# Another order for the attention blocks, other owners for the zeroing, and later stores, in an attention and mixture-of-experts kernel

## The chip, the cores and the metric

The program runs on one core of one Trainium2 chip. The metric is the device time of one execution in microseconds (us). A change is called faster or slower from 0.5% on, which is 4.5 us here.

## What is computed

The reference is an attention over short windows, a mixture of eight experts with a greedy assignment, and a gated network. Shapes: 4 batches, 8 heads, 768 positions, 64 elements in a head; 3072 tokens of 512 elements; expert width 1024.

```python
for c in range(24):                       # chunks of 32 queries
    k_full = concat([mem_k, k[16 to the left .. 8 to the right of the chunk]])   # 64 keys
    a = softmax(scale * q_c @ k_full.T)
    out[chunk] = a @ v_full
x = out.transpose(0, 2, 1, 3).reshape(3072, 512)
...
logits = x @ w_gate                       # pairs (token, expert) taken in falling order,
...                                       # each expert takes 384 tokens
for e in range(8):
    out[mask] = relu(x[mask] @ w1[e]) @ w2[e]
...
h = (x @ w1) * (x @ w2) @ w3
out = h @ w_out
```

## The kernel before

**Stages.** Attention comes first. It is cut into 32 units; unit u is half of a group g = u // 2 (one batch, one pair of heads, three tiles of 128 queries). One unit is a score block on TensorE (L298, 12 matmuls of 32 output partitions each), a maximum and a subtraction on VectorE (L308 to L312), an exponential on ScalarE (L316), a block of three transposes (L324) and its copy (L331), a value block (L341, again 12 matmuls of 32 output partitions), a division (L349 to L351), and a second block of three transposes with a copy (L324, L358). When four units have been done, a logit block follows (L372, 4 matmuls of 32 output partitions, and L381, three transposes). Score, value and logit blocks use 32 columns of the array, four blocks of columns side by side (column-tiled); transposes and all other matmuls use the full 128. A fp32 matmul of these blocks appears twice in the trace, so that a block of 12 is a row x24.

Then the tokens are assigned to experts (`route`, one pass for each expert: VectorE compares with thresholds, L569, and TensorE counts, L634 and L641). Beside the first pass TensorE multiplies `w3` with `w_out` ahead of time: 192 matmuls (L486, called combine matmuls here; 24 for each of 8 results) whose operands come from a conversion of 16 `w3` loads and 8 `w_out` loads on ScalarE and VectorE (L445 to L466). The first pass ends in a list of tokens; GpSimd gathers their rows (L812), and the eight experts follow one behind the other (L472 to L474 and L910 to L959).

**What sets the order.** `Plan` is a list scheduler that runs when the program is built. Each task asks for an engine ("P" TensorE, "V" VectorE, "A" ScalarE, "G" GpSimd, "D" the DMA issues of SyncE), a planned duration and an earliest time; `run` takes the task that could start first, by its own clock, and emits it. The order of the instructions on every engine is fixed by that. The planned durations have no other effect.

**Buffers and queues.** Keys lie in `kd0` to `kd2`, values in `vd0` to `vd2`, queries in `a5` to `a7`, for group g in buffer g % 3. The key and value buffers hold zeros outside two diagonal blocks, written once by memsets (L232). All loads and stores that matter here are issued by SyncE in order. `w3` blocks are loaded into `a6`, `a7`, `a5` (once the last scores of that query buffer are done) and into `a0` to `a4` (once the last logits are done). `stores` writes the attention's result to memory (`xs`), 24 stores of 128 tokens, from where it is gathered.

Of the kernel before, what the change touches and what calls it, by code (L numbers as in the profile page):

```python
# [11 lines left out]
I32 = mybir.dt.int32  # L12
# [48 lines left out]
GROUPS = B * HP  # L61
UNITS = 2 * GROUPS


class Slots:

# [30 lines left out]
class Plan:  # L97
# [8 lines left out]
    DMA = 2.3  # L106
    BIAS = 1.0

    def __init__(self):
        self.free = {e: 0.0 for e in "PVAGD"}  # L110
        self.at, self.tasks = {}, []

# [15 lines left out]
    def run(self):  # L128
        while self.tasks:
            ready = []  # L130
            for t in list(self.tasks):
                if t[2] is None:
                    self.step(t, None)
                if t[2] is None:
                    continue
                engines, held, _, after = t[2]
                held = held if isinstance(held, tuple) else (held,)
                e, h = min(zip(engines, held), key=lambda x: max(self.free[x[0]], after + self.LATENCY) + x[1] + (self.BIAS if x[0] == "V" else 0.0))
                ready.append((max(self.free[e], after + self.LATENCY), t[0], e, h, t))
            first = min(ready, key=lambda r: r[:2])  # L140
            same = [r for r in ready if r[2] == first[2] and r[0] <= first[0] + (self.SLACK if r[1] == 50.0 and r[2] == "V" else 0.0)]
            start, _, e, h, t = min(same, key=lambda r: (r[1], r[0]))
            emit = t[2][2]
            emit(e) if isinstance(t[2][1], tuple) else emit()
            self.free[e] = start + h
            self.step(t, start + h + (self.DMA if e == "D" else 0.0))


class Net:
# [78 lines left out]
    def zeros(self):  # L228
        nc = self.nc

        def zero(t, s):
            return lambda e: (nc.vector if e == "V" else nc.gpsimd).memset(t[:, s], 0.0)  # L232

        for i in range(3):
            for n, t in (("zk", self.KD[i]), ("zv", self.VD[i])):
                c = t.shape[2] * (t.shape[3] if len(t.shape) > 3 else 1) / 960
                t0 = yield ("VG", (c, c), zero(t, 0), 0.0)
                t1 = yield ("VG", (c, c), zero(t, 1), 0.0)
                self.at[n, i] = max(t0, t1)

    def loads(self):
        nc, io = self.nc, self.io

        def keys(g):
            b, hp = divmod(g, HP)
            if g >= 3:
                yield from self.wait(("s", 2 * g - 5))
            r = yield from self.wait(("zk", g % 3))

            def k():  # L250
                for s in range(2):
                    nc.sync.dma_start(self.KD[g % 3][s::2, s], io["kT"][b, hp, s])

            yield from queries(g) if g < 3 else ()
            t = yield ("D", 1.4, k, r)
            if g < 3:
                self.at["k", g] = t
            else:
                yield from queries(g)

        def values(g):
            b, hp = divmod(g, HP)
            r = yield from self.wait(("zv", g % 3) if g < 3 else ("o", 2 * g - 5))

            def v():
                for s in range(2):
                    nc.sync.dma_start(self.VD[g % 3][s::2, s].rearrange("p c d -> p (c d)"), io["vw"][b, hp, s])

            self.at["v", g] = yield ("D", 2.22, v, r)

        def queries(g):
            b, hp = divmod(g, HP)
            r = (yield from self.wait(("s", 2 * g - 5))) if g >= 3 else 0.0
            self.at["k", g] = yield ("D", 1.09, lambda: nc.sync.dma_start(self.Q[g % 3], io["qT"][b, hp]), r)

# [8 lines left out]
    def unit(self, u):  # L284
# [7 lines left out]
        p = bank[:, :6 * SL].rearrange("p (t h s) -> p t h s", t=3, h=2)  # L292

        def scores():
            for t in range(3):
# [4 lines left out]

        ts = at["s", u] = yield ("P", 0.89, scores, max(t0, tk))
        te, n = yield from self.EX.get()
# [4 lines left out]
        def top():  # L307
# [7 lines left out]
        P = self.P[n_P]  # L315
        t = yield ("A", 0.41, lambda: nc.scalar.activation(  # L316
            P.rearrange("p t (s h) -> p t h s", h=2), self.ex[n].rearrange("p (t h s) -> p t h s", t=3, h=2), AF.Exp, scale=0.125),
# [17 lines left out]
        o = bank[:, :6 * VW].rearrange("p (t h d) -> p t h d", t=3, h=2)  # L335

        def values():
            for t in range(3):
# [4 lines left out]

        t = at["o", u] = yield ("P", 0.89, values, max(t, to, tv))
        self.PTT.put(n_T, t)
# [16 lines left out]
    def logits(self, b, hf):  # L362
# [5 lines left out]
        tb, p = yield from self.R.get()  # L368

        def first():  # L370
            for k in range(HP):
# [18 lines left out]
    def stores(self, b, hf):  # L390
        t = yield from self.wait(*[("x", 2 * (HP * b + hp) + hf) for hp in range(HP)])
        for j in range(3):
            r = b * S + (3 * hf + j) * 128
# [33 lines left out]
    def fetch(self, jobs, *first):  # L427
        nc = self.nc
        yield from self.wait(*first)
        for n, tag, src, keys in jobs:  # L430
            t = yield from self.wait(*keys)
            raw = self.raw[n] = tag, self.place(tag, [1024], I32)
            self.at["raw", n] = yield ("D", 1.46, lambda: nc.sync.dma_start(raw[1], src.bitcast(I32)), t)

# [656 lines left out]
```

## Time and profile before

| | |
|---|---|
| median of 3 runs | 896.81 us (895.02 to 898.84) |
| profiled execution | 893.84 us, span 892.1 us |
| TensorE busy | 862.7 us (97% of the span) |
| VectorE busy | 579.7 us (65%) |
| ScalarE busy | 346.5 us (39%) |
| GpSimd busy | 65.3 us (7%) |

The span is the time from the first to the last instruction in the trace; the profiled execution is the same run with what lies around it. In the trace PE is TensorE, PEld its weight loads, DVE VectorE, ACT ScalarE, POOL GpSimd and SPq the DMA issues of SyncE. Ends of matmuls are modelled, so where one block follows another the start-to-start distance says what the first cost.

### The profile page before, as it was taken

Reading aid. Unit: us, or ns where it says so; the run is one execution under the profiler, and the core shown is the slowest. Engines: PE = TensorE matmul, PEld = TensorE weight load, DVE = VectorE, ACT = ScalarE, POOL = GpSimd, SP = SyncE. Lnnn points to the kernel's source line nnn. Section 1 sums busy time; section 2 is a strip of 40 time slices with the busy share of each in tenths; the row PEclk is TensorE's granted clock in tenths of the full one; section 3 lists DMA queues with packets and bytes.
Section 4 is the critical chain, followed back from the end, with each engine's and each line's share of the span. In section 5 each row is a group of like instructions: output and inputs, shape, how many; then the busy total and the mean of one; then the engine's idle time right before and its main releaser. Section 6 shows DMA issues by size and latency. Waiting matters only on the chain.

```text
span 892.1 us, 16212 instructions
## 1 busy us (share of the span) xinstructions
PE 862.7 (97%) x6561; PEld 776.5 (87%) x6561; DVE 579.7 (65%) x1321; ACT 346.5 (39%) x609; POOL 65.3 (7%) x88
## 2 busy tenths in 40 slices
PE   7999999899989999999999999999999999999996
PEld 6777667798979988998999999989999999999995
DVE  6889788697858856885779477857851175213211
ACT  3778796796223312331133113221341134113211
POOL 3000000000100010101011001100110011001001
PEclk9999999999999999999999999999999999999999
DMA  8999792850522160326023402530250024003000
GB/s 300 411 346 396 277 366 82 309 213 1 163 68 105 60 169 1 107 72 159 1 106 113 117 1 107 151 79 1 84 177 1 1 105 155 1 1 107 1 1 35
DMA packets 36267, 110.36 MB, mean 124 GB/s; under 512 B 9440, under 2 KB 9952, under 8 KB 35552
## 3 DMA queue, kind: packets, MB, share of 16 engines
q1 hardware_dynamic: 32352, 96.74, 31.6%
q0 software_dynamic: 3840, 12.59, 4.4%
q8 instruction: 51, 0.84, 0.4%
q14 instruction: 24, 0.20, 0.1%
HBM read 96.24 MB, written 13.07 MB: 123 GB/s over the span
## 4 chain that ended last, share of the span: by engine, by line
PE 78%; DVE 10%; DMA 7%; POOL 1%; issue 1%; ACT 1%; SPq 0%; POOLq 0%; DVEq 0%; ACTq 0%
PE bank L910 9%; PE bank L472 9%; PE bank L918 9%; PE bank L911 9%; PE bank L473 9%; PE bank L474 9%; PE bank L951 5%; PE bank L959 5%; PE bank L952 5%; DMA x<-xs,ix 4%; PE bank L486 3%; PE bank L634 2%; PE bank L324 1%; DVE kd L398 1%; DVE ex L756 1%; DMA a<-in_qT 1%
## 5 line engine op out<-in xcount | busy, mean ns | idle before, releaser
L472 PE MATMUL bank<-x,kd 128*128 128x384 f32 x512 | 175.8, 343 | 0.1
L473 PE MATMUL bank<-x,kd 128*128 128x384 f32 x512 | 172.5, 337 | 1.2 <-DVE kd L398 1.2
L474 PE MATMUL bank<-x,kd 128*128 128x384 f32 x512 | 172.3, 337 | 0.0
L936 DVE TENSOR_TENSOR pt<-pt,bank 128x384 f32<-128x384 f32 x64 | 35.3, 552 | 111.2 <-PE bank L918 104.2
L473 PEld LDWEIGHTS bank<-x,kd 128*128 128x128 f32 x512 | 96.5, 189 | 2.9 <-DVE kd L398 2.3
L472 PEld LDWEIGHTS bank<-x,kd 128*128 128x128 f32 x512 | 96.6, 189 | 1.1 <-ACT x L832 0.4
L474 PEld LDWEIGHTS bank<-x,kd 128*128 128x128 f32 x512 | 96.4, 188 | 0.3 <-DVE x L398 0.3
L666 DVE TENSOR_SCALAR_CACHE_REDUCE ex<-cv,thf 128x1536 bf16<-128x1536 f32 x50 | 90.4, 1809 | 0.3
L910 PE MATMUL bank<-x,a 128*128 128x384 f32 x256 | 87.9, 343 | 0.0
L929 ACT ACTIVATE pt<-bank 128x384 f32<-128x384 f32 x64 | 31.5, 492 | 145.3 <-PE bank L918 142.1
L910 PE MATMUL bank<-x,b 128*128 128x384 f32 x256 | 87.4, 341 | 0.0
L911 PE MATMUL bank<-x,a 128*128 128x384 f32 x256 | 86.0, 336 | 0.0
L911 PE MATMUL bank<-x,b 128*128 128x384 f32 x256 | 85.8, 335 | 0.0
L940 ACT ACTIVATE x<-pt 128x384 fp32r<-128x384 f32 x64 | 33.5, 524 | 123.0 <-DVE pt L936 120.7
L951 PE MATMUL bank<-vd,x 128*128 128x512 f32 x192 | 77.3, 402 | 0.4 <-ACT x L940 0.4
L952 PE MATMUL bank<-vd,x 128*128 128x512 f32 x192 | 75.9, 395 | 0.0
L959 PE MATMUL bank<-vd,x 128*128 128x512 f32 x192 | 66.6, 400 | 0.1
L873 ACT ACTIVATE x<-bank 128x384 fp32r<-128x384 f32 x64 | 31.3, 490 | 86.3 <-PE bank L474 78.5
L812 POOL DMA_INDIRECT x<-xs,ix x24 | 31.1, 1295 | 403.6 <-DVE e L593 143.4
L398 DVE TENSOR_TENSOR kd<-x,kd 128x1024 fp32r<-128x1024 f32 (+1 forms) x38 | 43.2, 1136 | 20.9 <-ACT kd L854 20.8
L918 PE MATMUL bank<-x,a 128*128 128x384 f32 x256 | 56.5, 339 | 0.0
L918 PE MATMUL bank<-x,b 128*128 128x384 f32 x256 | 55.1, 336 | 0.0
(157 smaller groups left out, 1524.1 us busy)
## 6 DMA issues: line engine op xcount, KB each, us to landing
p<-in_w SPq DMA_DIRECT2D x32, 512.0 KB, 3.6
x<-in_w SPq DMA_DIRECT2D x32, 512.0 KB, 3.6
vd<-in_vw SPq DMA_DIRECT2D x32, 390.0 KB, 7.2
a<-in_w SPq DMA_DIRECT2D x16, 512.0 KB, 7.2
kd<-in_kT SPq DMA_DIRECT2D x32, 246.0 KB, 6.2
cv<-vs SPq DMA_DIRECT2D x5, 1536.0 KB, 13.6
a<-in_qT SPq DMA_DIRECT2D x16, 384.0 KB, 6.3
xs<-x SPq DMA_DIRECT2D x24, 256.0 KB, 5.0
```

What stands on the lines that cost most here:

```text
L398: self.nc.vector.tensor_tensor(lo, src, hi.bitcast(F32), op=OP.subtract)
L472: mm(out, sh, mh, start=first, stop=False)
L473: mm(out, sl, mh, start=False, stop=False)
L474: mm(out, sh, ml, start=False, stop=last)
L666: tv = yield ("V", 0.14 + m / 960, lambda: V.tensor_scalar(self.cb[:, :m], self.vt[:, m * i:m * i + m], ti.bitcast(F32), None, op0=OP.is_g ...
L910: mm(q, w[:, 0, 128 * c:128 * c + 128], self.yT[0][:, c], start=(c == 0), stop=False)
L911: mm(q, w[:, 1, 128 * c:128 * c + 128], self.yT[0][:, c], start=False, stop=False)
L918: mm(q, w[:, 0, 128 * c:128 * c + 128], self.yT[1][:, c], start=False, stop=(c == KT - 1))
L936: t = yield ("V", 0.47, lambda: nc.vector.tensor_tensor(self.gf, self.ta, p1[:, :CAP], op=OP.mult), max(t, t1))
L951: mm(p, g[:, 0, r], wc[:, 0], start=(m == 0), stop=False)
L952: mm(p, g[:, 0, r], wc[:, 1], start=False, stop=False)
L959: t = yield ("P", DM * COL, lambda: mm(p, g[:, 1, r], wc[:, 0], start=False, stop=(m == FT - 1)), t1)
```

## The change

Column-tiled emitters get a mark. When the scheduler picks a TensorE task it adds 0.25 us to the start of one that would change between tiled and full (`SWITCH`), and it prefers an attention task (priority under 50) over a later one when that could start within 0.25 us. The planned duration of score and value blocks goes from 0.89 to 0.66, and some planned DMA and exponential durations change. The later key and value buffers are zeroed by GpSimd alone; of the first pair VectorE and GpSimd zero one half each. The stores of batches 1 to 3 wait, in the plan, for the last values' load.

```diff
+def tiled(emit):
+
+    emit.tiled = True
+    return emit
...
+    SWITCH = .25
...
+                turn = self.SWITCH if e == "P" and self.tiled != getattr(t[2][2], "tiled", False) else 0.0
-                ready.append((max(self.free[e], after + self.LATENCY), t[0], e, h, t))
+                ready.append((max(self.free[e], after + self.LATENCY) + turn, t[0], e, h, t))
             first = min(ready, key=lambda r: r[:2])
+            if first[2] == "P" and first[1] > 50.0:
+                first = min((r for r in ready if r[2] == "P" and r[0] <= first[0] + self.SWITCH and r[1] < 50.0), default=first,
+                            key=lambda r: r[:2])
...
-                t0 = yield ("VG", (c, c), zero(t, 0), 0.0)
-                t1 = yield ("VG", (c, c), zero(t, 1), 0.0)
+                t0 = yield ("G" if i else "V", (c,), zero(t, 0), 0.0)
+                t1 = yield ("G", (c,), zero(t, 1), 0.0)
...
-            t = yield ("D", 1.4, k, r)
+            t = yield ("D", 1.3, k, r)
...
-            self.at["v", g] = yield ("D", 2.22, v, r)
+            self.at["v", g] = yield ("D", 2.05, v, r)
...
+        @tiled
         def scores():
...
-        ts = at["s", u] = yield ("P", 0.89, scores, max(t0, tk))
+        ts = at["s", u] = yield ("P", 0.66, scores, max(t0, tk))
...
-        t = yield ("A", 0.41, lambda: nc.scalar.activation(
+        t = yield ("A", 0.48, lambda: nc.scalar.activation(
...
+        @tiled
         def values():
...
-        t = at["o", u] = yield ("P", 0.89, values, max(t, to, tv))
+        t = at["o", u] = yield ("P", 0.66, values, max(t, to, tv))
...
+        @tiled
         def first():
...
         t = yield from self.wait(*[("x", 2 * (HP * b + hp) + hf) for hp in range(HP)])
+        if b:
+            yield from self.wait(("v", GROUPS - 1))
...
-            self.at["raw", n] = yield ("D", 1.46, lambda: nc.sync.dma_start(raw[1], src.bitcast(I32)), t)
+            self.at["raw", n] = yield ("D", 1.35, lambda: nc.sync.dma_start(raw[1], src.bitcast(I32)), t)
```

**TensorE, in the middle of attention.** Before (L298 scores, L341 values, L324 transposes, the bank and the operands behind the name):

```order
L324 MATMUL bank5_106<-ident_73,p_24_99 128x128 x3
L324 MATMUL bank4_105<-ident_73,x2_17_92 128x128 x3
L298 MATMUL bank2_103<-kd1_2_77,a6_13_88 32x128 x12
L324 MATMUL bank5_106<-ident_73,x3_18_93 128x128 x3
L298 MATMUL bank0_101<-kd1_2_77,a6_13_88 32x128 x12
L341 MATMUL bank6_107<-vd0_4_79,pt_25_100 32x130 x12
L324 MATMUL bank4_105<-ident_73,p_24_99 128x128 x3
L324 MATMUL bank5_106<-ident_73,p_24_99 128x128 x3
L298 MATMUL bank1_102<-kd2_3_78,a7_14_89 32x128 x12
L341 MATMUL bank7_108<-vd0_4_79,pt_25_100 32x130 x12
L324 MATMUL bank4_105<-ident_73,x2_17_92 128x128 x3
L324 MATMUL bank5_106<-ident_73,p_24_99 128x128 x3
```

The same place in the changed kernel, where L313 is the score, L357 the value and L339 the transpose line:

```order
L339 MATMUL bank5_106<-ident_73,p_24_99 128x128 x3
L313 MATMUL bank2_103<-kd1_2_77,a6_13_88 32x128 x12
L313 MATMUL bank0_101<-kd1_2_77,a6_13_88 32x128 x12
L357 MATMUL bank7_108<-vd2_6_81,pt_25_100 32x130 x12
L339 MATMUL bank4_105<-ident_73,x3_18_93 128x128 x3
L339 MATMUL bank5_106<-ident_73,x2_17_92 128x128 x3
L339 MATMUL bank4_105<-ident_73,p_24_99 128x128 x3
L339 MATMUL bank5_106<-ident_73,p_24_99 128x128 x3
L313 MATMUL bank1_102<-kd2_3_78,a7_14_89 32x128 x12
L357 MATMUL bank6_107<-vd0_4_79,pt_25_100 32x130 x12
L357 MATMUL bank7_108<-vd0_4_79,pt_25_100 32x130 x12
L313 MATMUL bank2_103<-kd2_3_78,a7_14_89 32x128 x12
```

In the rows of before the array changes between tiled and full 6 times, in those of the changed kernel 3 times; counted over the whole TensorE order there are 86 changes before and 48 now, with the same blocks.

**TensorE, at the end of attention.** Before, from the transposes of the last two units' probabilities on (L486 is the first combine matmul):

```order
L324 MATMUL bank5_106<-ident_73,p_24_99 128x128 x3
L324 MATMUL bank4_105<-ident_73,p_24_99 128x128 x3
L324 MATMUL bank5_106<-ident_73,x6_21_96 128x128 x3
L341 MATMUL bank6_107<-vd0_4_79,pt_25_100 32x130 x12
L324 MATMUL bank4_105<-ident_73,x7_22_97 128x128 x3
L341 MATMUL bank7_108<-vd0_4_79,pt_25_100 32x130 x12
L324 MATMUL bank5_106<-ident_73,x6_21_96 128x128 x3
L486 MATMUL bank2_103<-b0_34_384,kd1_54_1612 128x512 x3
```

And now (L505 is the combine line):

```order
L339 MATMUL bank4_105<-ident_73,p_24_99 128x128 x3
L339 MATMUL bank5_106<-ident_73,p_24_99 128x128 x3
L505 MATMUL bank2_103<-b0_34_378,kd1_52_1524 128x512 x3
L505 MATMUL bank2_103<-b1_36_569,kd1_52_1524 128x512 x2
L339 MATMUL bank4_105<-ident_73,x6_21_96 128x128 x3
L357 MATMUL bank6_107<-vd0_4_79,pt_25_100 32x130 x12
L357 MATMUL bank7_108<-vd0_4_79,pt_25_100 32x130 x12
L339 MATMUL bank5_106<-ident_73,x7_22_97 128x128 x3
```

Five combine matmuls have moved ahead of the last two value blocks. Further on, 18 instead of 16 combine matmuls stand ahead of the last logit transposes (L381), 36 in both ahead of the second count (L634), and 36 instead of 39 ahead of that count's flag (L641); 168 instead of 159 ahead of the second row product (L763) of the first assignment, and 24 instead of 31 between that and the transposes of the gathered rows.

**SyncE, around the last values' load.** Before, from the last values' load to the first `w3` load behind the stores (L267 values, L433 `w3` with its buffer, L394 stores with the tile stored):

```order
L267 DMA vd0_4_79<-in_vw 64x1560 x2
L433 DMA a6_46_1324<-in_w3 128x1024
L433 DMA a7_50_1532<-in_w3 128x1024
L433 DMA a5_51_1566<-in_w3 128x1024
L394 DMA xs_66<-x0_15_90 128x512 x3
L394 DMA xs_66<-x1_16_91 128x512 x3
L394 DMA xs_66<-x2_17_92 128x512 x3
L394 DMA xs_66<-x3_18_93 128x512 x3
L394 DMA xs_66<-x4_19_94 128x512
L433 DMA a0_57_1690<-in_w3 128x1024
```

And now (L281 values, L452 `w3`, L413 stores):

```order
L452 DMA a7_48_1400<-in_w3 128x1024
L281 DMA vd0_4_79<-in_vw 64x1560 x2
L452 DMA a5_50_1470<-in_w3 128x1024
L413 DMA xs_66<-x0_15_90 128x512 x3
L413 DMA xs_66<-x1_16_91 128x512 x3
L413 DMA xs_66<-x2_17_92 128x512 x3
L413 DMA xs_66<-x3_18_93 128x512 x3
L413 DMA xs_66<-x4_19_94 128x512 x3
L413 DMA xs_66<-x5_20_95 128x512 x3
L413 DMA xs_66<-x6_21_96 128x512 x3
L413 DMA xs_66<-x7_22_97 128x512 x2
L452 DMA a0_57_1706<-in_w3 128x1024
```

Two `w3` loads (into `a6` and `a7`) now stand ahead of the last values' load, and 23 stores instead of 13 stand between the load into `a5` and the load into `a0`; the 12 `w3` loads after that follow directly in both, and the stores that are left follow those.

## Rows read from the trace of the kernel before

**Rows 1.** The page's chain that ended last: share of the span by engine.
```profile
PE 78%; DVE 10%; DMA 7%; POOL 1%; issue 1%; ACT 1%; SPq 0%; POOLq 0%; DVEq 0%; ACTq 0%
```

**Rows 2.** Stretches: length, busy us of PE, PEld, DVE, ACT, POOL, granted clock, DMA share, GB/s.
```profile
40.00:60.00 20.00, 19.63 (x423) 15.08 (x419) 17.45 (x57) 16.04 (x33) 0.00 (x0) 1.00 1.01 389
...
100.00:120.00 20.00, 18.53 (x125) 12.67 (x124) 14.20 (x35) 15.75 (x28) 0.00 (x0) 0.91 0.87 337
...
200.00:300.00 100.00, 97.27 (x626) 88.51 (x626) 77.13 (x177) 37.60 (x65) 7.34 (x9) 1.00 0.25 75
```

**Rows 3.** Timeline of PE in attention: start, us, instructions.
```profile
41.14 0.86 PE L298 MATMUL bank<-kd,a 128*32 128x128 f32 x24
41.93 0.55 PE L381 MATMUL bank<-ident,a 128*128 128x128 f32 x3
42.32 0.82 PE L324 MATMUL bank<-ident,x 128*128 128x128 f32 x6
43.06 1.54 PE L341 MATMUL bank<-vd,pt 128*32 128x130 f32 x48
44.42 0.84 PE L298 MATMUL bank<-kd,a 128*32 128x128 f32 x24
```

**Rows 4.** Waits of PEld, 20 to 100 us: total us, times, longest.
```profile
PEld bank L324 <- issue: 3.4, 15, 0.6
...
PEld bank L298 <- issue: 2.9, 17, 0.2
```

**Rows 5.** Timeline of PE at the end of attention, with idle time before.
```profile
97.00 0.52 PE L324 MATMUL bank<-ident,x 128*128 128x128 f32 x3 [1.46 <-DVE small L350]
97.45 0.87 PE L341 MATMUL bank<-vd,pt 128*32 128x130 f32 x24
...
107.00 0.49 PE L381 MATMUL bank<-ident,a 128*128 128x128 f32 x3
```

**Rows 6.** Timeline of SyncE's DMA issues, 79 to 123 us.
```profile
79.63 5.08 SPq L267 DMA_DIRECT2D vd<-in_vw  x4
84.75 7.96 SPq L433 DMA_DIRECT2D a<-in_w  x3
92.75 9.46 SPq L394 DMA_DIRECT2D xs<-x  x13
105.85 16.93 SPq L433 DMA_DIRECT2D a<-in_w  x13
```

**Rows 7.** DMA issues to 170 us: times, KB each, median us to landing.
```profile
vd<-in_vw SPq DMA_DIRECT2D x32, 390.0 KB, 7.2
a<-in_w SPq DMA_DIRECT2D x16, 512.0 KB, 7.2
```

**Rows 8.** Timeline of PE beside the first assignment and at the gather.
```profile
114.78 0.93 PE L634 MATMUL bank<-M,ex 128*63 128x8 bf16 x24 [1.33 <-DVE ex L569]
115.64 1.03 PE L486 MATMUL bank<-b,kd 128*128 128x512 f32 x3
...
151.32 0.46 PE L763 MATMUL bank<-mv,ex 128*128 128x6 bf16 x12
151.64 7.36 PE L486 MATMUL bank<-b,kd 128*128 128x512 f32 x31
...
162.34 1.31 PE L828 MATMUL bank<-ident,x 128*128 128x128 f32 x10 [3.13 <-DMA x<-xs,ix]
```

**Rows 9.** Timeline of DVE: the fourth `w3` block's conversion ends.
```profile
114.65 0.68 DVE L398 TENSOR_TENSOR kd<-cv,kd 128x512 fp32r<-128x512 f32 x1
```

**Rows 10.** Source line of the memsets, then timeline: third key load, its first use.
```profile
L232 POOL MEMSET kd<- x3: 911/911/912, 1.3 to 5.7; 128x984 f32 x3
L232 POOL MEMSET vd<- x3: 1391/1391/1392, 2.1 to 6.5; 128x1560 f32 x3
...
10.15 1.48 SPq L252 DMA_DIRECT2D kd<-in_kT  x2
...
17.10 1.28 PE L298 MATMUL bank<-kd,a 128*32 128x128 f32 x24 [1.97 <-DMA vd<-in_vw]
```

More of the change, by code (lines that the diff above doesn't have):

```diff
@@ L107 @@
     BIAS = 1.0
+    SWITCH = .25
     def __init__(self):
         self.free = {e: 0.0 for e in "PVAGD"}
+        self.tiled = False
         self.at, self.tasks = {}, []
@@ L145, in run @@
             self.free[e] = start + h
+            if e == "P":
+                self.tiled = getattr(t[2][2], "tiled", False)
             self.step(t, start + h + (self.DMA if e == "D" else 0.0))
@@ L273, in queries @@
             r = (yield from self.wait(("s", 2 * g - 5))) if g >= 3 else 0.0
-            self.at["k", g] = yield ("D", 1.09, lambda: nc.sync.dma_start(self.Q[g % 3], io["qT"][b, hp]), r)
+            self.at["k", g] = yield ("D", 1.0, lambda: nc.sync.dma_start(self.Q[g % 3], io["qT"][b, hp]), r)
         yield from keys(0)
```

## Prediction

> **What bounds the kernel now.** I read the chain that ended last first: 78% of it is TensorE [rows 1]. The table of stretches then says where TensorE is short of work: behind the first gather it is busy 97.27 of 100 us and has almost nothing to give [rows 2]. So the change must pay ahead of about 165 us, in attention, beside the first assignment, or at the gather. In attention four things run near their limits together: from 40 to 60 us TensorE is busy 19.63 of 20 us, VectorE 17.45, ScalarE 16.04, and the DMA share is 1.01 [rows 2]. The timeline of TensorE shows what the busy figure hides, the cost of a change between tiled and full blocks [rows 3]. Last come the SyncE issues [rows 6] and the places where TensorE stands still: 1.46 us at the end of attention [rows 5], 1.33 us ahead of the second count, and 3.13 us for the gathered rows [rows 8].
>
> **The change, part by part.** Sums are made against the profiled execution, 893.84 us, which is 3.0 us under the median 896.81; I add the result to the median.
>
> *Fewer changes of tiling: -4.2 us.* In rows 3 two tiled blocks in one row (43.06 to 44.42) take 1.36 us to the next start, so 0.68 each. A tiled block ahead of a full one takes 41.93 - 41.14 = 0.79: the change costs 0.11. Three transposes cost between 0.82 - 0.55 = 0.27 (what three more add to a row) and 42.32 - 41.93 = 0.39 us (from one full block to the next), 0.33 in the middle; the six at 42.32 take 0.74 to the next tiled start, so the change back costs between nothing and 0.20, about 0.10. I take 0.11 for either. The orders have 86 and 48 changes: 38 x 0.11 = 4.2 us. The other end is what the weight loads sit idle: 3.4 / 15 = 0.23 us ahead of full blocks and 2.9 / 17 = 0.17 ahead of tiled ones [rows 4], mean 0.20, or 38 x 0.20 = 7.6 us. Part of that gap lies under the matmuls in flight, and the start-to-start distance holds all that the engine pays, so I take the lower. Below 4.2 us, down to nothing, it falls only if TensorE then waits for loads (rival C).
>
> The Trainium skill, "TensorEngine Tiling", section Tiling Modes, says that a change of mode drains the engine. "TensorE: Matmul & The Clock Gate", section Single matmul latency, gives a constant part of 166 ns for one matmul alone on a warm clock; if a drain costs that, an estimate by this page is 38 x 0.166 = 6.3 us, and the whole sum below would be -3.5 us instead of -1.4. The row shows less than the page's figure, and the sum goes by the row.
>
> *Combine matmuls moved ahead of the last value blocks: -1.2 us.* Before, TensorE waits 1.46 us there for VectorE [rows 5]. Five combine matmuls now stand in that place; one takes 7.36 / 31 = 0.237 us [rows 8], together 1.2 us of work that no longer has to be done later. It needs the first `w3` block early: its load now stands ahead of the last values' load, whose row waits and takes 5.08 us for four issues [rows 6]; two of those are passed, so about 2.5 us earlier. If the block is late, the value blocks queue behind it, and this term turns from a gain of 1.2 into a loss of the same size.
>
> *Stores ahead of most w3 loads: +2.3 us.* SyncE issues in order. Before, 13 stores take 9.46 us, 0.73 each; then the load into `a0` waits until the logits have been read, and goes out at 105.85, 13.1 us behind the end of the load into `a5` at 92.71 [rows 6]. Now 23 stores take 23 x 0.73 = 16.8 us, with no wait for the logits, so `a0` is 3.6 us later measured from `a5`. The load into `a5` waits for the last score block. Between that block and the last logit transposes TensorE now has more to do than before: six transpose blocks and two logit transposes (0.33 each), a value block and a logit block (0.68 each) and two combine matmuls (0.24 each), 4.5 us, less the 1.5 us wait that is filled. So at most 3 us of the 3.6 are made up, and fewer if small waits shrink too, down to about 0.5; I take the middle, 1.8, which leaves 1.8. The fourth `w3` block, out of `a0`, was ready at 114.65 + 0.68 = 115.33, and its first matmul ran at 115.64 [rows 8, 9]: no slack. So these 1.8 us become a wait of TensorE. Two combine matmuls fewer between the last logit transposes and the second count (18, not 20) leave another 0.5 us open, since VectorE's comparison already ends last there (1.33 us) [rows 8]. Queued behind the waiting combine matmul is the third count, so the assignment waits too. Below: nothing, if ScalarE gets through its conversions sooner. Above: rival D.
>
> *Gather: +1.7 us.* From the last row product (151.32 + 0.46 = 151.78) to the gathered rows at 162.34 there are 10.6 us, filled with 31 combine matmuls but for 3.13 us [rows 8]. Now 24 are left to fill it: 7 x 0.237 = 1.7 us more idle. Those matmuls are done earlier, and that time has been counted as work in its new place.
>
> *Zeroing by GpSimd: 0.* GpSimd now clears, from 1.3 us on, five key halves and five value halves; the last key half is done at 1.3 + 5 x 0.91 + 3 x 1.39 = 10.0 us, and the third key load goes out at 10.15 anyway [rows 10]. The second key load cannot go out whole ahead of 1.3 + 3 x 0.91 + 1.39 = 5.4 us, which may hold it by up to 1 us. VectorE is free some 5 us sooner, but TensorE stands still until 17.10 for the loads that follow [rows 10]; that wait covers both a gain and the loss. Without the cover it is worth 1 us either way.
>
> *After the gather: 0.* The work is the same and TensorE is busy 97 of 100 us; the order differs a little in every expert, and I give it 1 us either way.
>
> Sum: -4.2 - 1.2 + 2.3 + 1.7 = **-1.4 us**, 892.4 in a profiled execution, **895.4 us** on the median.
>
> **The rivals.** *B, the full price of a change.* If the idle of the weight loads is what a change costs (7.6 us) and the `w3` blocks arrive in time: -7.6 - 1.2 + 1.7 = -7.1, 889.7 us. For it: the gaps stand in rows 4 under "issue", which waits for nothing else. Against it: the distance of 0.79 us in rows 3.
>
> *C, the loads set attention's pace.* Then the 4.2 us become waits for keys and values: -1.2 + 2.3 + 1.7 = +2.8, 899.6 us. For it: DMA share 1.01 in rows 2, with VectorE at 87%. Against it: the last values were issued by 84.71 us, landed about 7.2 us later at 91.9 [rows 6, 7], and were used at 97.45 [rows 5], 5.5 us of slack that 4.2 us does not use up.
>
> *D, w3 blocks late; the side of slower.* The place is the first matmul out of `a0`. If none of the ten added stores' 10 x 0.73 = 7.3 us is made up, because the stores keep the DMA engines filled and the `w3` loads land only behind them (7.2 us is the median [rows 7]), TensorE waits 7.3 us there. A clock loss comes with it: in the stretch with the 1.33 us wait the granted clock was 0.91 over 20 us, a loss of 1.8 us [rows 2, 8]; one such again. Then -4.2 - 1.2 + 1.7 + 7.3 + 1.8 = +5.4, 902.2 us. It decides (slower by 4.5) from a wait of 6.4 us on. Against it: TensorE's 4.5 us of added work in between.
>
> **How the numbers follow.** The forecast has a chance of 0.42, with a range of its own of 892 to 898.5 us (1 us either way for what follows the gather, and the 0.5 to 3 us above). B has 0.28, C 0.14, D 0.16. A measurement of this kernel tells a change of 0.5%, 4.5 us, from none: under 892.3 is faster, over 901.3 slower. B and 0.05 of the forecast's low tail make 0.33 for faster, D 0.16 for slower, the rest, with C, 0.51 for the same. The range reaches into B and up to C: 889 to 900.5 leaves out about 0.1 of B and most of D, 2 in 10.
>
> **What would show it.** The last logit transposes should start 3 to 6 us ahead of 107.00; a tiled block ahead of a full one should still take 0.79 us. The first combine matmul should start without a wait for its weights. The load into `a0` should go out between 103 and 107 us, and the third count should wait for a combine matmul whose weights VectorE has just written. The wait for the gathered rows should be near 5 us, and they should arrive at 160 to 162 us. The forecast is wrong if attention ends no sooner (C), if it ends 7 us sooner with no wait behind it (B), if the wait at `a0` exceeds 6 us (D), or if experts 1 to 7 differ by more than 1 us together, of which these rows say nothing.

## The result, and the profile after

The changed kernel takes 909.93 us (median of 4 runs, 906.34 to 911.80) against 895.91 us before: ratio 1.0149, 95% interval 1.0105 to 1.0193, 14 us slower. Its profiled execution took 906.34 us, span 904.6 us against 892.1. TensorE was busy 864.8 us (862.7 before): the time was lost in waiting and at a lower granted clock. The traces below are those of these two executions, 12.5 us apart in span.

Stretches of the changed kernel, columns as in [rows 2]:

```profile
40.00:60.00 20.00, 18.89 (x410) 15.40 (x410) 16.83 (x56) 15.25 (x33) 0.00 (x0) 1.00 1.00 394
100.00:120.00 20.00, 18.06 (x179) 11.96 (x174) 12.90 (x37) 12.73 (x24) 0.00 (x0) 0.99 1.02 390
200.00:300.00 100.00, 96.73 (x658) 86.75 (x657) 76.94 (x176) 43.44 (x75) 7.47 (x9) 1.00 0.27 75
...
60.00:70.00 10.00, 7.42 (x149) 6.08 (x145) 6.22 (x17) 5.25 (x11) 0.00 (x0) 0.83 1.01 404
120.00:130.00 10.00, 9.14 (x49) 6.38 (x49) 6.82 (x20) 8.93 (x16) 0.00 (x0) 0.67 1.01 382
165.00:175.00 10.00, 4.85 (x20) 3.84 (x20) 4.08 (x6) 4.04 (x8) 0.95 (x1) 0.66 1.02 410
```

In mid-attention (40 to 60 us) TensorE has lost 0.74 us of work against [rows 2]. In the last three stretches TensorE was busy 9.31, 10.00 and 10.00 us before, at a granted clock of 1.00. One of these losses is in part an old one that moved: before, the clock was low from 110 to 120 us, where it is 0.99 now.

```profile
110.00:120.00 10.00, 8.66 (x68) 6.44 (x66) 8.30 (x20) 9.47 (x16) 0.00 (x0) 0.83 1.00 397
```

TensorE in attention, where [rows 3] showed no gap:

```profile
30.05 1.13 PE L357 MATMUL bank<-vd,pt 128*32 128x130 f32 x30
32.17 0.85 PE L357 MATMUL bank<-vd,pt 128*32 128x130 f32 x18 [0.99 <-issue]
...
46.72 0.87 PE L339 MATMUL bank<-ident,x 128*128 128x128 f32 x6
47.84 0.93 PE L339 MATMUL bank<-ident,p 128*128 128x128 f32 x6 [0.25 <-ACT a L374]
...
60.70 1.47 PE L313 MATMUL bank<-kd,a 128*32 128x128 f32 x42
64.75 0.42 PE L313 MATMUL bank<-kd,a 128*32 128x128 f32 x6 [2.58 <-issue]
```

Two kinds of stop. In the middle of a tiled block TensorE stands still while no semaphore holds it ("issue"): after the 30th of 48 value matmuls, after the 42nd of 48 score matmuls. And of four transpose blocks in a row, on two banks, the third waits until ScalarE has copied the first. TensorE's longest waits from 20 to 110 us:

```profile
PE bank L313 <- issue: 3.6, 2, 2.6
PE bank L339 <- ACT a L374: 2.5, 5, 1.2
PE bank L339 <- ACT pt L346: 2.1, 4, 0.9
PE bank L357 <- issue: 1.0, 1, 1.0
```

Before, the same view had 1.6 us for ScalarE and no "issue" line. SyncE, and TensorE from the end of attention to the gathered rows, in answer to [rows 5, 6, 8]:

```profile
92.84 16.41 SPq L413 DMA_DIRECT2D xs<-x  x23
110.90 13.96 SPq L452 DMA_DIRECT2D a<-in_w  x12
```

```profile
100.68 1.56 PE L505 MATMUL bank<-b,kd 128*128 128x512 f32 x5
...
111.54 0.55 PE L398 MATMUL bank<-ident,a 128*128 128x128 f32 x3
...
118.92 0.93 PE L653 MATMUL bank<-M,ex 128*63 128x8 bf16 x24 [1.31 <-DVE ex L588]
...
121.02 4.93 PE L505 MATMUL bank<-b,kd 128*128 128x512 f32 x10 [0.67 <-ACT kd L484]
...
159.38 0.46 PE L782 MATMUL bank<-mv,ex 128*128 128x6 bf16 x12
159.70 5.75 PE L505 MATMUL bank<-b,kd 128*128 128x512 f32 x24
168.46 0.47 PE L847 MATMUL bank<-ident,x 128*128 128x128 f32 x1 [3.01 <-DMA x<-xs,ix]
170.08 0.47 PE L847 MATMUL bank<-ident,x 128*128 128x128 f32 x1 [1.15 <-DMA x<-xs,ix]
171.55 2.39 PE L847 MATMUL bank<-ident,x 128*128 128x128 f32 x10 [0.99 <-DMA x<-xs,ix]
173.60 0.67 PE L491 MATMUL bank<-x,kd 128*128 128x384 f32 x1
```

And the first expert matmul before:

```profile
163.96 0.34 PE L472 MATMUL bank<-x,kd 128*128 128x384 f32 x1
```

The last logit transposes start 4.5 us later than in [rows 5], the second row product 8.1 us later than in [rows 8], the first expert matmul at 173.60 instead of 163.96 us, 9.6 us later; the last 2.9 us of the 12.5 in span come behind it.

### The profile page after: what moved, and what is told of

Its sections match the earlier page's. It is cut to its first block, busy times and chain, and to the rows that moved or that the text cites. A ratio compares the mean times of both kernels' runs of the same rounds, so it can differ in the third digit from the quotient of the medians.

```text
span 904.6 us, 16213 instructions
## 1 busy us (share of the span) xinstructions
PE 864.8 (96%) x6561; PEld 780.2 (86%) x6561; DVE 574.5 (64%) x1317; ACT 346.4 (38%) x609; POOL 71.6 (8%) x92
## 4 chain that ended last, share of the span: by engine, by line
PE 72%; DMA 9%; DVE 9%; ACT 5%; issue 2%; POOL 2%; SPq 0%; POOLq 0%; ACTq 0%; DVEq 0%
PE bank L929 9%; PE bank L937 9%; PE bank L930 9%; PE bank L491 7%; PE bank L492 7%; PE bank L493 6%; DMA x<-xs,ix 5%; PE bank L970 5%; PE bank L978 5%; PE bank L971 5%; PE bank L505 4%; DVE ex L685 2%; DVE kd L417 2%; DMA b<-in_wo 1%; PE bank L313 1%
## 5 line engine op out<-in xcount | busy, mean ns | idle before, releaser
L994 POOL DMA_INDIRECT out<-x,ix x24 | 24.5, 1022 | 432.1 <-ACT x L989 429.0
```

## The experiments

Theories. T1: in long tiled runs TensorE runs out of instructions while loads fill the DMA engines. T2: grouped value blocks come late, values loads wait for them and hold SyncE. T3: the `w3` loads behind 23 stores. T4: the zeroing or the planned durations. T5: transposes in a row wait for ScalarE, because conversions stand ahead of its copies (T5a) or because two banks are too few (T5b). The stores' wait needs no run: the changed kernel built without it has the same order, instruction for instruction.

Results, with the changes of tiling, the start of the last logit transposes, and TensorE's idle time from 20 us to there as the sum of the timeline's entries for "issue" and for ScalarE. Each ratio is taken against runs of the kernel before from the same session, whose medians lie between 894.88 and 895.91 us:

| kernel | changes | median us | ratio to before, 95% | last logits us | issue, ScalarE us |
|---|---|---|---|---|---|
| before | 86 | 895.91 | | 107.00 | 0, 1.6 |
| changed | 48 | 909.93 | 1.0105 to 1.0193 | 111.54 | 4.6, 4.9 |
| e1 ungrouped | 92 | 897.05 | 1.0007 to 1.0053 | 108.26 | 1.4, 0.9 |
| e2 group alone | 42 | 904.23 | 1.0071 to 1.0145 | 115.37 | 1.4, 6.1 |
| e3 old zeroing | 42 | 904.99 | 1.0076 to 1.0134 | 108.96 | 1.4, 5.3 |
| e4 zeroing alone | 86 | 894.40 | 0.9984 to 1.0024 | 108.77 | 1.5, 2.3 |
| e5 values by GpSimd | 48 | 912.21 | 1.0145 to 1.0199 | 112.44 | 2.3, 3.3 |
| e6 stores behind w3 | 48 | 906.42 | 1.0094 to 1.0145 | 111.48 | 4.2, 5.1 |
| e7 cap full | 54 | 907.44 | 1.0098 to 1.0157 | 114.91 | 2.1, 7.5 |
| e8 cap both | 74 | 898.31 | 1.0014 to 1.0056 | 110.07 | 1.3, 6.1 |
| e10 short conversions | 48 | 906.17 | 1.0105 to 1.0158 | 112.54 | 5.1, 3.4 |
| e11 third bank, grouped | 38 | 899.04 | 1.0019 to 1.0058 | 107.02 | 4.0, 3.3 |
| e12 third bank, before | 86 | 899.90 | 1.0034 to 1.0072 | 106.48 | 2.2, 2.6 |
| e13 short copies, grouped | 48 | 908.02 | 1.0115 to 1.0167 | 109.43 | 5.1, 2.2 |
| e14 short copies, before | 86 | 895.80 | 0.9992 to 1.0031 | 110.88 | 1.7, 1.1 |
| e15 third bank, group alone | 34 | 906.44 | 1.0098 to 1.0176 | 110.64 | 3.7, 3.7 |
| e16 third bank, small price | 44 | 903.16 | 1.0054 to 1.0110 | 109.29 | 3.9, 2.3 |
| e17 light loads, grouped | 48 | 898.92 | 1.0017 to 1.0060 | 102.21 | 0, 0.7 |
| e18 light loads, before | 86 | 895.51 | 0.9975 to 1.0022 | 107.51 | 0, 0.9 |

### Which part of the change (e1 to e4)

e1 takes the grouping out of the changed kernel; e2 is the grouping alone; e3 and e4 exchange the zeroing.

```diff
# e1
-    SWITCH = .25
+    SWITCH = 0.0
-            if first[2] == "P" and first[1] > 50.0:
-                first = min(...)
# e3, on the changed kernel; e4 is the reverse on the kernel before
-                t0 = yield ("G" if i else "V", (c,), zero(t, 0), 0.0)
-                t1 = yield ("G", (c,), zero(t, 1), 0.0)
+                t0 = yield ("VG", (c, c), zero(t, 0), 0.0)
+                t1 = yield ("VG", (c, c), zero(t, 1), 0.0)
```

> The changed kernel without the grouping alone: the planner neither charges a change of tiling nor prefers a block below priority 50, and the planned durations, the zeroing and the stores' wait stay; 92 changes of tiling instead of 48. Four theories. T1: in long tiled runs TensorE runs out of instructions while data loads fill the DMA engines; then this kernel has no idle of more than 0.8 us inside a tiled block between 20 and 100 us and takes 896 to 899 us. T2: grouped value blocks come late, so the values loads wait for them and SyncE, which issues in order, lets the DMA engines run dry; then the DMA share from 70 to 80 us is above 0.9 here, and the time is 896 to 899 us as well. T3: attention is not the matter, the w3 loads behind the stores are; here 11 stores stand ahead of most of them instead of 23, so T3 gives 899 to 903 us with the last logit transposes still at 110 to 112. T4: the new zeroing or the new planned durations cost the time; then 905 to 910 us.

> The kernel before with the grouping alone (price of a change 0.25, preference, marks); planned durations, zeroing and stores as before; 42 changes of tiling and tiled runs of up to 11 blocks. T1: idle of 1 us or more inside tiled blocks while the DMA share is about 1, 3 to 6 us in all, time 903 to 910 us. T2: a row of SyncE that waits over 4 us for a value block, DMA share under 0.7 in the 10 us behind it, time 903 to 910 us. T3: 22 stores stand ahead of most w3 loads, but six of them are issued ahead of the last values' loads, so the load into a0 comes about 4 us earlier than in the changed kernel: 900 to 904 us. T4: as before, 894 to 898 us.

> The changed kernel with the zeroing of the kernel before (VectorE or GpSimd by the earlier planned start); behind the first 16 blocks TensorE's order is that of the changed kernel. T1, T2 and T3: 906 to 911 us, as the changed kernel, to 1.5 us either way. T4 by the zeroing: 897 to 900 us.

> The kernel before with the new zeroing alone; TensorE's order behind the first blocks and SyncE's order are those of before. T1, T2 and T3: 894.5 to 898.5 us, as before, since TensorE stands still until 17 us for the loads in any case. T4 by the zeroing: 903 us or more.

The grouping alone costs 1.08%, 9.7 us. Without it 0.3% is left, 2.7 us (0.6 to 4.7). I put that down to the planned durations, since the zeroing alone is worth nothing (e4), but no run has the durations alone. e1 has one stop of 1.07 us inside a tiled block, where T1 expected none over 0.8. In e2 the stops under "issue" are 1.4 us, not the 3 to 6 that T1 expected, beside 6.1 us for ScalarE: which wait limits differs from one grouped order to the next. e3 lies 5 us under the changed kernel, but their intervals overlap. T4 falls for the zeroing and may hold for a small part by the durations.

### The values loads, the stores, the length of the runs (e5 to e8)

```diff
# e5
-                    nc.sync.dma_start(self.VD[g % 3][s::2, s]...
+                    (nc.sync if g < 3 else nc.gpsimd).dma_start(self.VD[g % 3][s::2, s]...
# e6
+        if b >= 2:
+            yield from self.wait(("raw", 3 * FT - 1))
# e7: self.turns counts full blocks in a row; e8: blocks of either kind
-turn = self.SWITCH if e == "P" and self.tiled != getattr(...) else 0.0
+turn = self.SWITCH if e == "P" and self.tiled != getattr(...) and self.turns < 2 else 0.0
```

> The changed kernel with one edit: from the fourth group on the values loads are issued by GpSimd, which has nothing else to do in attention, instead of SyncE. TensorE's, VectorE's and ScalarE's orders are those of the changed kernel, instruction for instruction. T2 (a values load that waits for a late value block holds SyncE, and the keys, queries and wo loads behind it): the loads behind it go out on time, the DMA share from 70 to 80 us is above 0.9 instead of 0.55, the last logit transposes start 3 to 5 us sooner, and the time is 902 to 906 us. T5 (four transpose blocks in a row need ScalarE to empty two banks, so TensorE waits for ScalarE, and ScalarE and VectorE stand still while TensorE does four tiled blocks): TensorE's waits for ScalarE from 20 us to the last logit transposes stay at 4 to 6 us, and the time is 907 to 911 us, as the changed kernel.

> The changed kernel, but the stores of the last two batches wait for the last w3 load: 12 stores stand ahead of most w3 loads instead of 23; TensorE's order up to the second count is unchanged. T3: the load into a0 goes out within 1 us of the logits being read, TensorE's waits around the second count (2.3 us in the changed kernel) shrink under 1 us, the granted clock from 120 to 130 us stays above 0.9 instead of 0.67, and the time is 902 to 906 us. If the loss is in attention (T2, T5): 906 to 910 us.

> The grouping alone, as in the second run, but a change of tiling is free once two full blocks stand in a row: 54 changes of tiling instead of 42, and half as many places with four transpose blocks in a row. T5: TensorE's waits for ScalarE between 20 us and the last logit transposes fall from 6.4 to 3 to 4.5 us, time 898 to 902 us. T2: value blocks still come in pairs behind pairs of score blocks, the SyncE waits stay, 902 to 906 us.

> The grouping alone, but a change is free once two blocks of one kind stand in a row, either kind: 74 changes instead of 86 before, the combine matmuls placed as before. T5 and T2 both say that the loss is gone: waits for ScalarE of 1.5 to 2.5 us, a values load that waits less than 4 us, 892.5 to 896.5 us. What 12 fewer changes give is 0.8 us at 0.07 us each, the price between the traces so far. If any grouping costs (not its length), 898 us or more.

T2 falls: with SyncE free the DMA share from 70 to 80 us rises from 0.55 to 0.89, and the time does not fall. T3 falls as put: in e6 the stores end at 100.75 us and the load into `a0` still goes out at 110.84, as in the changed kernel at 110.90; it waits for the logits, not for the stores. What e6 does change is the clock behind it, since three combine matmuls now stand between the second count and its flag:

```profile
120.00:130.00 10.00, 9.70 (x90) 7.16 (x88) 9.04 (x23) 10.00 (x19) 0.00 (x0) 1.00 0.95 364
```

That may be worth up to 3 us, which the intervals do not tell apart. e7 and e8 both came out over the ranges of T2 and T5. In the orders so far the loss grows with the grouping: 0.35% at 74 changes, 1.1 to 1.5% at 42 to 54. e8 still waits 6.1 us for ScalarE and is 9 us faster than e7, so these waits alone do not make the loss.

### The price of a change, alone (e9)

TensorE by itself, blocks of both kinds in runs of 1, 2, 4 and 8:

```diff
+            for run in (1, 2, 4, 8):
+                for block in (score, value):
+                    for _ in range(48 // run):
+                        for _ in range(run):
+                            block()
+                        for _ in range(run):
+                            turn()
+                    mark()
```

> The price of a change of tiling by itself. TensorE alone, out of constants, with no wait for anything: 48 score blocks and 48 blocks of three transposes in runs of 1, then the same with value blocks, then both in runs of 2, of 4 and of 8; 96, 48, 24 and 12 changes per stretch. It leaves out everything else of the computation. The prediction's price of 0.11 us a change gives 10.6 us between runs of 1 and an order without changes, so 9.2 us between runs of 1 and of 8; 0.07 us, as between the traces so far, gives 5.9 us; 0.20 us, the idle of the weight loads, 16.8 us.

Timeline of TensorE in e9: start of each stretch with score blocks, and of the mark that ends it.

```profile
44.73 0.74 PE L98 MATMUL bank<-kd,q 128*32 128x128 f32 x18
...
105.59 1.02 PE L110 MATMUL bank<-wide,p 128*128 128x512 f32 x2
...
168.85 0.42 PE L98 MATMUL bank<-kd,q 128*32 128x128 f32 x7
...
222.84 1.02 PE L110 MATMUL bank<-wide,p 128*128 128x512 f32 x2
...
279.22 0.54 PE L98 MATMUL bank<-kd,q 128*32 128x128 f32 x12
...
329.74 1.02 PE L110 MATMUL bank<-wide,p 128*128 128x512 f32 x2
```

60.86, 53.99 and 50.52 us with 96, 48 and 24 changes: 0.143 and 0.145 us a change. So 38 changes are worth 5.5 us of TensorE's time, not 4.2. There is no idle entry in e9's timeline from 45 us on, in runs of 8 blocks either: long runs do not stop TensorE when nothing is loaded.

### ScalarE's copies and the banks (e10 to e16)

```diff
# e10: first three steps of the wo conversions
+        z = 64 if n < FT else 512
+        high, byte = high[:, :z], byte[:, :z]
# e11, e12, e15, e16: a third bank for the transposes, until the last logits are read
-        self.W, self.R = Slots(bank[0:3]), Slots(bank[3:4])
-        self.T, self.O = Slots(bank[4:6]), Slots(bank[6:8])
+        self.W, self.R = Slots(bank[0:3]), Slots([])
+        self.T, self.O = Slots(bank[3:6]), Slots(bank[6:8])
# e13 on the changed kernel, e14 on the kernel before; the same for XT
-activation(PT.rearrange("p t k -> p (t k)"), bank[:, :384], AF.Copy)
+activation(PT[:, 0], bank[:, :128], AF.Copy)
```

> The changed kernel, but ScalarE's first three steps of each wo conversion (24 instructions of 0.7 to 0.8 us, all in attention) take 64 of 512 columns; the rest of those weights is left out and stands for zeros. TensorE's order is that of the changed kernel, ScalarE has about 13 us less to do in attention. T5a (ScalarE comes late to the transposed banks because conversions stand ahead of the copies): TensorE's waits for ScalarE fall from 4 to 5 us to under 2, the last logit transposes start 2 to 4 us sooner, 905 to 908 us. T5b (the copy of two banks itself is the loop: four transpose blocks in a row on two banks): waits for ScalarE of 3.5 to 5 us, 908 to 912 us.

> The changed kernel with a third bank for the transposes in attention (the logits' bank joins them and goes back behind the last logits); 38 changes of tiling, four transpose blocks in a row still. T5b: TensorE's waits for ScalarE in attention under 2.5 us, time 899 to 904 us. If long runs cost in another way (values late, instructions, the combine matmuls and the clock behind attention): 906 to 912 us.

> The kernel before with the same third bank, without grouping; 86 changes. If its few waits for ScalarE (1.6 to 2.3 us) go, 892 to 894.5 us; if nothing else moves, 894 to 897 us; combine matmuls left for the wait for the gathered rows are 24 instead of 31, which costs up to 1.7 us.

> The changed kernel, but ScalarE copies 128 of the 384 columns out of each transposed block, 64 copies in attention; the other columns stay zeros, so part of attention and of the logits is left out. TensorE's and SyncE's orders are those of the changed kernel. T5b (four transpose blocks in a row on two banks wait for ScalarE's copies): TensorE's waits for ScalarE fall from 4 to 5 us to under 1.5, the last logit transposes start 3 to 5 us sooner than 111.5, 902 to 906 us. If the runs cost in another way: 907 to 911 us.

> The same cut in the kernel before, as a control: the same part left out, TensorE's order that of before. T5b: its waits for ScalarE are 1.6 to 2.3 us, so at most 2 us can go: 892.5 to 895.5 us. If ScalarE's copies hold TensorE whatever the order, it gains as much as the grouped order does, 4 us or more: under 891.5 us.

> The grouping alone with the third bank for the transposes, planned durations and zeroing as before: a second order with long runs, 34 changes and tiled runs of up to 14 blocks. If the third bank is what mends the changed kernel: 896 to 901 us, against 904.2 with two banks. If the first one was a lucky order: 903 to 909 us.

> As the run before, with a planned price of 0.03 instead of 0.25 for a change, 44 changes, runs of up to 9 blocks. Third bank mends it: 896 to 901 us, and if the price alone of 0.144 us a change counted, 1.4 us behind the 34 changes. Long runs cost in another way: 903 us or more.

T5a falls: in e10 the time lies in its range, but the waits for ScalarE are 3.4 us instead of under 2 and attention ends no sooner. e11 looked like T5b, but its waits for ScalarE were 3.3 us instead of under 2.5, and two more orders with the third bank (e15, e16) are 7 to 11 us slower than before; why e11's order comes out better stays open. e12 has no grouping and is still 0.5% slower than before, over its range, and it too has only 24 combine matmuls left for the gather. e13 decides with the order fixed: the waits for ScalarE fall from 4.9 to 2.2 us, attention ends 2.1 us sooner, and the time does not move outside its interval. T5b is real, but small. What is left in e13 is "issue" (waits of TensorE from 20 to 108 us, and one of the places):

```profile
PE bank L317 <- issue: 3.9, 3, 2.0
PE bank L343 <- ACT pt L350: 1.3, 3, 0.9
PE bank L361 <- issue: 1.2, 2, 0.8
```

```profile
61.42 1.47 PE L317 MATMUL bank<-kd,a 128*32 128x128 f32 x42
64.92 0.42 PE L317 MATMUL bank<-kd,a 128*32 128x128 f32 x6 [2.03 <-issue]
```

It is the place of the changed kernel's longest stop, again after the 42nd of 48 matmuls. Counted in matmuls from the start of the trace, the stops lie at 471, 596 and 1101 in the changed kernel, at 471, 596, 849, 975 and 1101 in e10 and e13 and, in other orders, at 852, 978 and 1105 (e11) and at 597 and 722 (e14), to one matmul: 125 to 127 apart (not 129, as the expectation of e17 has it), or a multiple, whatever stands there. e9 moved 82 packets, 1.34 MB, on the DMA queue for instructions, for 20,928 instructions of TensorE: 255 for one packet, which is 127 matmuls with their weight loads. TensorE stops at the edges of its instruction packets.

The traces list these packets one by one. This is the one of the longest stop (packets, MB, share of 16 engines, 62.4 to 63.6 us):

```profile
q8 instruction: 1, 0.02, 5.7%
```

It began to move at 62.45 us, when TensorE had already stopped. The packets of the three stops took 0.99, 1.08 and 1.10 us, those of e9 0.88 to 1.45, so what comes late is the start of a packet, not its end. In no kernel of the table does TensorE go over an edge in attention less than 2.2 us behind the start of its packet (edges counted on at 126 matmuls a packet). In the changed kernel it goes over all seven edges from 25 to 65 us 2.3 to 2.6 us behind, so there it went as fast as its instructions came. In the trace of the kernel before the same seven lie 3.15 to 3.92 us behind.

### Lighter loads (e17, e18)

```diff
-nc.sync.dma_start(self.VD[g % 3][s::2, s].rearrange("p c d -> p (c d)"), io["vw"][b, hp, s])
+nc.sync.dma_start(self.VD[g % 3][s::2, s].rearrange("p c d -> p (c d)")[:, :NC * VW // 2], io["vw"][b, hp, s][:, :NC * VW // 2])
...
+            z = 128 if n < FT else 1024
```

> The changed kernel with the shortened copies of the run before last but three, and lighter loads: the values loads bring half of their columns and the eight wo loads an eighth; the rest stands for zeros, so parts of attention and of the weights are left out. TensorE's order is that of the changed kernel. The load queue then is less full. T1, as the traces now put it: TensorE's instructions come in packets of 16 KB through the same DMA engines, one per 256 TensorE instructions; the stalls under no releaser fall on every 129th matmul, always there, and only while the DMA share is about 1. Then these stalls (4 to 5 us between 20 and 70 us in the order with runs) fall under 1.5 us, attention ends at 103 to 106 instead of 109.4 to 111.5 us, and the time is 899 to 904 us. If they stay at 4 us or more at the same matmuls, the loads do not matter: 906 to 909 us.

> The same cuts in the kernel before, as a control, TensorE's order that of before. It stalls 0 to 1.7 us without a releaser, so the lighter loads give 0 to 2 us: 893 to 896 us, and attention ends at 106 to 110 us. With both waits out of the way, the grouped order's attention (without the combine matmuls in it) should be ahead of this one by up to 38 changes at 0.144 us, 5.5 us. If the grouped order is still not ahead, a third wait is open.

The stretch from 20 to 65 us in the changed kernel, in e17 and in e18:

```profile
20.00:65.00 45.00, 38.45 (x882) 30.70 (x880) 35.48 (x110) 32.36 (x66) 0.00 (x0) 1.00 1.02 404
```

```profile
20.00:65.00 45.00, 42.73 (x1012) 35.23 (x1008) 39.69 (x124) 30.42 (x73) 0.08 (x1) 1.00 0.89 295
```

```profile
20.00:65.00 45.00, 44.03 (x944) 33.18 (x945) 38.24 (x116) 28.82 (x71) 3.46 (x4) 1.00 0.79 259
```

TensorE's order in e17 is that of the changed kernel. With the DMA share at 0.89 instead of 1.02 every "issue" stop is gone, TensorE does 1012 matmuls in these 45 us instead of 882 (879 in e13), attention ends at 102.21 us, 7.2 us ahead of e13, and the time falls by 9.1 us. In the order before the same relief is worth 0.3 us of time (e18 against e14). So it is the grouped order that the full load queue slows. Now its attention ends 5.3 us ahead of the ungrouped one, part of which is that e18's first value block starts at 17.81 instead of 12.81 us. e17 is still 3.4 us behind e18, and loses it behind attention: 62.5 instead of 57.2 us from the last logit transposes to the first expert matmul, with 24 instead of 31 combine matmuls left for the gather, and in these traces 734.6 instead of 727.8 us behind that.

The packets fit this. From the start of the first of the seven to that of the last it is 39.2 us in the changed kernel, 37.3 in the kernel before and 32.7 in e17: with full loads the grouped order got its instructions no faster than the ungrouped one.

## Why the prediction was wrong

**Fewer changes: the step that failed.** The term said that 4.2 us less work on TensorE end attention 4.2 us sooner, and that this falls "only if TensorE then waits for loads". The price was too low, 0.144 us measured against 0.11. The Trainium skill, "TensorEngine Tiling (Array Packing)", section Tiling Modes, with its drain, and the 166 ns of "TensorE: Matmul & The Clock Gate", section Single matmul latency, gave an estimate of 6.3 us; e9 measures 5.5, nearer to that than to my rows. The error is in what follows: the freed time became waits. From 20 us to the last logits they grew from 3.7 to 10.0 us: 4.6 for instructions that had not arrived, 3.2 more for ScalarE's copies, 1.5 less for VectorE; and the clock fell to 0.83 from 60 to 70 us, around the 2.58 us stop. So attention ended 4.5 us later, not 4.2 us sooner. The waits, 0.5 us for two more combine matmuls and at most 1.7 us for the clock, less the 5.5 us saved, make about 3 of the 4.5 us; the rest is open. Rival C had the DMA share of 1.01 as its argument and looked for late keys and values. These were in time; late were TensorE's own instructions. In the trace of before there was nothing to see of it: there the packets came 3.15 us or more ahead of use. That the full load queue slows the grouped order is shown (e17 against e13, e18 against e14). That it does so by the instruction packets is shown for the stops, by their places, their going and the late starts of the packets; the other waits that went with them are not split up, and in e2 the waits for ScalarE are the larger part.

**Combine matmuls ahead of the last value blocks: right.** The five start at 100.68 us without a wait, and the 1.46 us of [rows 5] are gone.

**Stores ahead of the `w3` loads: right sign, wrong reason.** The load into `a0` went out at 110.90 us, not 103 to 107, because the logits were late (e6). The matmul whose weights are late waits 0.67 us, for ScalarE's part of the conversion and not VectorE's; the second count waits 1.31 us, as before. The larger cost was the clock, 0.67 from 120 to 130 us: ten combine matmuls take 4.93 us instead of the 2.4 that ten by [rows 8] take. By the granted clocks from 100 to 130 us this stretch loses about 3.5 us now and lost 1.8 before. Rival D's wait of 7.3 us did not come, its clock loss did. From the last logit transposes to the second row product it is 47.8 instead of 44.3 us.

**Gather: right, and not whole.** 24 combine matmuls are left, and the waits for the rows are 3.01, 1.15 and 0.99 us, 5.15 together, as forecast near 5. The rows are there from 168.5 us on, not at 160 to 162, since all ahead of them is later. But behind these waits the granted clock falls to 0.66 from 165 to 175 us, with a DMA share of 1.02 from the next loads; that was not in the sum. From the second row product to the first expert matmul it is 14.2 instead of 12.6 us. This goes with the number of combine matmuls left, not with the grouping or the planned durations as such: the kernels with 31 left take 12.5 to 13.2 us, but for e11 with 14.4, and those with 22 to 26 left take 14.2 to 15.9, among them e12, ungrouped and with the old durations.

**Zeroing: right** (e4). **Behind the gather:** 731.0 instead of 728.1 us from the first expert matmul to the end, beyond the 1 us given. Profiled executions of these kernels lie between 726.0 (e4) and 736.8 us (e5) there, so what the order adds stays open.

The range was too narrow on the slow side because each wait was priced where the trace of before had one. Attention's limit was not one engine but four things at their limit, as the prediction itself read from [rows 2], and a gain on one of them was booked in full. None of the versions beats the kernel before.

## What to carry to other kernels

Where engines and DMA are all near their limit, less work on the longest engine is not a gain until the others can follow: ask what must arrive faster, its instructions among it. Many small matmuls in a row are the quickest use of instructions: a tiled block takes 48 of them in 0.68 us, three transposes 6 in 0.33 us. A stop without a releaser inside a block, beside a DMA share near 1, asks first for a look at the instruction queue's packets and for lighter loads there. And when planned durations change, compare how the filler work ahead of the known waits has moved: in e1, without any grouping, 23 instead of 31 were left for the gather, and it was 2.7 us slower.

## What the runs showed of the hardware

- TensorE's instructions come over the DMA engines in packets of 16 KB (1.34 MB in 82 packets in e9), one for 255 instructions. With the DMA share at 1.02 a packet's edge inside a tiled block cost up to 2.58 us; at 0.89, and in e9, nothing. TensorE's order of before, which uses its instructions more slowly, lost nothing (before), 1.5 us (e4) and 1.7 us (e14) at such edges.
- The Trainium skill, "DMA: Bandwidth & Descriptors", section SWDGE vs HWDGE vs iDMA, says that a DMA engine takes its 16 internal queues in turn. By that an instruction packet would have to wait for little more than a packet of the load queue. The stops of 1 to 2.6 us, which go when the loads are lighter, do not fit that well. The traces place the loss ahead of the packet's start; whether the packet was asked for late or stood in line, no run here shows.
- A change between tiled and full blocks costs 0.143 to 0.145 us by itself, the same in runs of 1, 2 and 4.
